# A feed-forward product of twin tiles in seven half products, with weight sums kept in DRAM

## The chip, the cores and the metric

One core of a Trainium2 chip runs the whole program; the metric is the device time of one execution in microseconds, and the median of several executions stands for a kernel. The core's engines are TensorE (matrix products into eight PSUM banks), VectorE and ScalarE (elementwise work), GpSimd (elementwise work) and SyncE, whose queue issues nearly all transfers between DRAM and SBUF. They run side by side and wait for each other by semaphores.

## The reference

Attention with a decay runs in blocks over 4 sequences of 768 tokens with 8 heads of 64; its output, 3072 tokens by 512, goes through a feed-forward part with a squared ReLU:

```python
intra = np.einsum('bhic,bhjc->bhij', qb, kb) * Dmask[None]
intra = np.einsum('bhij,bhjd->bhid', intra, vb)
inter = np.einsum('bhid,bhde->bhie', qb * lam_pow[None], kv_state)
out[:, :, sl] = intra + inter
...
h = np.maximum(x @ w_in, 0.0)
return (h * h @ w_out).astype(np.float32)
```

x is 3072 x 512, w_in 512 x 2048, w_out 2048 x 512. All inputs and the output are 32-bit floats.

## The kernel before

The tokens are cut into 24 chunks of 128. SIZES puts them into seven tiles of 3 or 4 chunks (tiles 0, 1, 3 and 5 have 3 chunks, 384 columns; tiles 2, 4 and 6 have 4, 512 columns). A tile's feed-forward part is 16 steps, one for each block f of 128 hidden features (`ffn`). Numbers are held as a rounded high part and a remainder, both in the fp32r type, so a product of two matrices is three products: high by high, high by low, low by high. A step is

- the first product (mm1, L654): the block's input weights wih and wil by the tile's halves xs, 4 groups of 128 rows times three products, 12 matmuls into one bank;
- on ScalarE the ReLU of that bank (L668) and its square, rounded, into gh (L674); on VectorE the square once more (L677) and the remainder gl (L679);
- the second product (mm2): for each chunk gh by woh (L660), gh by wol (L661), gl by woh (L663), added over the 16 steps into one bank per chunk, which stays open for the tile.

In tiles 0 and 1 ScalarE squares in place (L671) and rounds with a cast (L672), and VectorE has the one subtraction. Buffers gh and gl exist twice. When a tile ends, its banks are copied to ob rows (L697) and stored (L699).

The weights come once, 32 pieces of 512 KB (L366), are turned from 64-bit to 32-bit floats on ScalarE and VectorE (L368 to L375) and split into their two halves; they then stay in SBUF. That work goes on beside tile 0 and the beginning of tile 1. Attention for chunks 6 to 23 is done in ten *visits* (VISITS: tile, step, steps ahead), a run of some 250 small matmuls (L393) that finishes two old chunks and opens two new ones between two steps of a tile; L410 loads q, k and v of a chunk. A finished chunk's result is scaled on VectorE into xr and split into the halves xs (L500, L501).

No engine's order is left to chance: a planner (`Plan.order`) takes operations with an estimated duration, a key (a due time), their dependences and the buffers they need, and puts each engine's instructions out in the order of its own simulation; each engine runs its queue in that order.

## Time and profile before

| | us |
|---|---|
| median of 3 executions | 597.36 |
| fastest and slowest of them | 597.3, 597.68 |
| span of the profiled execution | 596.8 |
| TensorE busy in it (share) | 590.8 (99%) |
| VectorE busy | 292.0 (49%) |
| ScalarE busy | 214.1 (36%) |
| GpSimd busy | 5.4 (1%) |

The span is what one profiled execution shows from its first to its last instruction; the median is measured without the profiler and is 0.6 us longer. In the profile, L12 stands for line 12 of the kernel, PE is TensorE, PEld its weight loads, DVE VectorE, ACT ScalarE, POOL GpSimd, and SP or SPq the queue of SyncE. Matmuls are pipelined and their single durations overlap, so the length of a step is read from the starts of steps. Busy time of an engine off the chain of waits costs nothing by itself.

### The profile page before, as it was taken

What the parts mean: (1) busy time and instruction counts of PE and PEld (TensorE: products, weight loads), DVE (VectorE), ACT (ScalarE), POOL (GpSimd) and SP (SyncE); (2) the same over time, 40 slices, a digit from 0 to 9 for tenths busy, and PEclk for the clock granted to TensorE, in tenths of its full rate; (3) what the DMA queues carried; (4) which work ended last, traced back from release to release, by engine and by line L of the source; (5) the groups of instructions that cost most, each with busy time, mean ns of one, the idle gap of its engine ahead of it and who ended that gap; (6) DMA issues with size and microseconds to landing.
All of it is one profiled execution on the core that took longest, in us unless ns stands there. A gap on an engine that the chain in (4) does not pass through costs nothing.

```text
span 596.8 us, 11701 instructions
## 1 busy us (share of the span) xinstructions
PE 590.8 (99%) x5097; PEld 512.7 (86%) x5097; DVE 292.0 (49%) x551; ACT 214.1 (36%) x427; POOL 5.4 (1%) x10
## 2 busy tenths in 40 slices
PE   8999999999999999999999999999999999999997
PEld 7789898999888888889899888888889998888885
DVE  6999999954563525332624433532232524313223
ACT  5876677653342222223322222221222322222122
POOL 3000000000000000000000000000000000000000
PEclk9999999999999999999999999999999999999999
DMA  8775444505450304001403010300010000100001
GB/s 331 293 260 176 142 158 160 177 1 195 143 193 12 136 0 144 0 22 50 144 0 128 15 54 0 144 0 1 0 72 0 3 0 2 53 1 0 1 0 71
DMA packets 15171, 48.99 MB, mean 82 GB/s; under 512 B 1809, under 2 KB 1809, under 8 KB 15121
## 3 DMA queue, kind: packets, MB, share of 16 engines
q1 hardware_dynamic: 14976, 48.24, 22.7%
q8 instruction: 40, 0.66, 0.4%
q14 instruction: 11, 0.08, 0.0%
q10 hardware_dynamic: 144, 0.01, 0.0%
HBM read 41.95 MB, written 6.29 MB: 81 GB/s over the span
## 4 chain that ended last, share of the span: by engine, by line
PE 95%; DMA 4%; SPq 0%; issue 0%; DVE 0%
PE bank L654 44%; PE bank L660 15%; PE bank L661 15%; PE bank L663 15%; PE bank L393 7%; DMA ka<-ka 2%; DMA qv<-qv 2%; PE bank L637 0%; SPq L410 0%; DVE work L697 0%; SPq L366 0%
## 5 line engine op out<-in xcount | busy, mean ns | idle before, releaser
L654 PE MATMUL bank<-xs,wih 128*128 128x384 f32 (+1 forms) x888 | 193.2, 359 | 0.5 <-issue 0.5
L654 PEld LDWEIGHTS bank<-xs,wih 128*128 128x128 f32 x888 | 161.0, 188 | 19.7 <-issue 1.0
L677 DVE TENSOR_TENSOR work<-work 128x512 f32<-128x512 f32 (+1 forms) x79 | 50.4, 638 | 231.8 <-ACT gh L674 231.8
L668 ACT ACTIVATE work<-bank 128x512 f32<-128x512 f32 (+1 forms) x86 | 47.4, 551 | 285.5 <-PE bank L654 234.9
L660 PE MATMUL bank<-woh,gh 128*128 128x512 f32 x381 | 149.7, 393 | 0.0
L661 PE MATMUL bank<-wol,gh 128*128 128x512 f32 x381 | 148.6, 390 | 0.0
L654 PE MATMUL bank<-xs,wil 128*128 128x384 f32 (+1 forms) x444 | 105.2, 359 | 0.0
L663 PE MATMUL bank<-woh,gl 128*128 128x512 f32 x336 | 92.4, 390 | 0.0
L654 PEld LDWEIGHTS bank<-xs,wil 128*128 128x128 f32 x444 | 80.6, 188 | 7.5
L660 PEld LDWEIGHTS bank<-woh,gh 128*128 128x128 f32 x381 | 71.5, 188 | 14.0
L661 PEld LDWEIGHTS bank<-wol,gh 128*128 128x128 f32 x381 | 71.5, 188 | 13.2
L663 PEld LDWEIGHTS bank<-woh,gl 128*128 128x128 f32 x336 | 62.9, 188 | 13.0
L679 DVE TENSOR_TENSOR gl<-work,gh 128x512 fp32r<-128x512 f32 (+1 forms) x87 | 55.0, 632 | 17.3 <-ACT gh L672 10.4
L674 ACT ACTIVATE gh<-work 128x512 fp32r<-128x512 f32 (+1 forms) x79 | 46.6, 590 | 2.5
L393 PE MATMUL bank<-qv,ka 64*64 64x64 f32 (+2 forms) x1040 | 26.5, 225 | 0.4 <-DMA qv<-qv 0.3
L393 PEld LDWEIGHTS bank<-qv,ka 64*64 64x64 f32 (+2 forms) x1040 | 23.7, 140 | 3.0 <-DMA qv<-qv 1.1
L373 DVE SCALAR_TENSOR_TENSOR work<-work 128x512 uint32<-128x512 uint32 x30 | 20.7, 690 | 0.4
L375 DVE SCALAR_TENSOR_TENSOR work<-work 128x512 uint32<-128x512 uint32 x30 | 20.7, 690 | 0.3
L668 ACT ACTIVATE ob<-bank 128x384 f32<-128x384 f32 (+1 forms) x25 | 12.4, 496 | 22.2 <-PE bank L654 21.2
L368 ACT ACTIVATE work<-work 128x512 f32<-128x512 f32 x30 | 20.2, 674 | 0.0
L500 ACT CAST xs<-xr 128x512 fp32r<-128x512 f32 x15 | 9.3, 620 | 17.4 <-DVE xr L493 15.2
L433 DVE TENSOR_TENSOR qv<-qv,wdec 128x512 f32<-128x512 f32 (+2 forms) x20 | 11.2, 562 | 8.5 <-DMA qv<-qv 8.3
(95 smaller groups left out, 401.5 us busy)
## 6 DMA issues: line engine op xcount, KB each, us to landing
work<-w SPq DMA_DIRECT2D x32, 512.0 KB, 3.5
ka<-ka SPq DMA_DIRECT2D x24, 512.0 KB, 5.2
qv<-qv SPq DMA_DIRECT2D x20, 512.0 KB, 5.7
out<-ob SPq DMA_DIRECT2D x16, 256.0 KB, 2.3
out<-work SPq DMA_DIRECT2D x8, 256.0 KB, 2.5
work<-qv SPq DMA_DIRECT2D x4, 512.0 KB, 6.7
ob<-lamx ACTq DMA_DIRECT2D x1, 10.0 KB, 4.5
```

The source lines that it names most:

```text
L368: o = add("ACT", 0.13 + act(n), lambda cs=cs: nc.scalar.activation(at(m)[:, cs], words(1, cs).bitcast(F32), AF.Abs), [o], [st, m])
L373: o = add("DVE", tt(n), lambda cs=cs: nc.vector.scalar_tensor_tensor(out=bits(cs), in0=words(1, cs), scalar=0xC0000000, in1=bits(cs), op0= ...
L375: om.append(add("DVE", tt(n), lambda cs=cs: nc.vector.scalar_tensor_tensor(out=bits(cs), in0=words(0, cs), scalar=29, in1=bits(cs), op0=AL ...
L393: nc.tensor.matmul(*args, **kw, skip_group_check=True)
L654: nc.tensor.matmul(at(h)[:, 0:n], wt[:, cc, :], xt[:, cc, :], start=k == 0, stop=k == 3 * NCC - 1)
L660: nc.tensor.matmul(at(os_[j]), at(gh)[:, sl], woh[f], start=f == 0 and ti >= SINGLE, stop=False)
L661: nc.tensor.matmul(at(os_[j]), at(gh)[:, sl], wol[f], start=False, stop=False)
L663: nc.tensor.matmul(at(os_[j]), at(gl)[:, sl], woh[f], start=False, stop=f == NF - 1)
L668: orr = plan.op("ACT", 0.49 * to - 0.03 * (nt > 3), key, lambda: nc.scalar.activation(raw(), at(h)[:, 0:n], AF.Relu), [o1], [h, g, run])
L674: ogh = plan.op("ACT", 0.525 * to - 0.03 * (nt > 3), key, lambda: nc.scalar.activation(high(), raw(), AF.Square), [orr], [g, gh])
L677: og = plan.op("DVE", 0.07 + n / 770, key, lambda: nc.vector.tensor_tensor(out=square(), in0=raw(), in1=raw(), op=ALU.mult), [orr] + [ogh] ...
L679: ogl = plan.op("DVE", 0.07 + n / 770, key, lambda: nc.vector.tensor_tensor(out=low(), in0=square(), in1=high(), op=ALU.subtract), [og, og ...
```

## The change

SIZES keeps the first three tiles (10 chunks). The other 14 chunks become two *twins*: the first has 3 pairs of chunks (narrow, 384 columns a side), the second 4 pairs (wide, 512 columns). One twin covers two former tiles, and two feature blocks are taken together. The first product of such a pair of blocks for both sides is a 2 by 2 product: features f0 and f1, sides a and b, with the 512 rows in two halves of 256. It is done in Strassen's way (Winograd's form) with seven products of half the rows, six matmuls each (ORDER gives their sequence, `product`), and sums of their results: z11 and z12 are blocks f0 and f1 for side a, z21 and z22 for side b (`run`). ScalarE copies a result out of its bank (`copy`, after's L841), VectorE adds the next bank to it (`plus`, L844).

The sums of the inputs that a twin needs are made by VectorE when a pair of chunks is ready (`pairs`) and split like the chunks. The sums of the weights are made once, by GpSimd (`differences`): for a pair of blocks two additions of high and low part (L766, 128 x 512) and four subtractions (L775, 128 x 256), in a row, then a cast to the high part on ScalarE (L777) and the remainder on VectorE (L778). The seven moving parts per pair of blocks (three of them plain weight halves) are stored in a DRAM tensor, kept, 256 KB each (L762), and every product of both twins loads its own back into one of six buffers (`load`, L825). So 56 parts, 14.7 MB, are stored, and each is read twice.

z11 and z12 are squared at once (`whole`) and their second products follow in the next round of the same first half of the twin. z21 and z22 are squared in place and kept in SBUF (`put`); a second half of the twin casts them again (`kept_half`, L910, L911) and does their second products (L891, L892, L894), with nothing but visits between. Six visits stay in tiles 1 and 2; four lie in the twins (INSIDE). Tile 2 now squares like tiles 0 and 1 (L731, L733, L734). SBUF is laid out by hand, since the twins' buffers lie where earlier ones were (REGIONS, ERAS; `Plan.follow` adds the dependences), and gh and gl still exist twice. The work of the ten visits, the conversion of the weights and tiles 0 and 1 are otherwise left as they were.

```diff
-SIZES = [3, 3, 4, 3, 4, 3, 4]
-WIDE, NARROW = max(SIZES) * C, min(SIZES) * C
+SIZES = [3, 3, 4]
+TWINS = [3, 4]
+WIDE, NARROW = 4 * C, 3 * C
...
+VISITS = [(1, 9, 0), (1, 12, 1), (1, 14, 0), (2, 5, 0), (2, 9, 0), (2, 13, 0)]
+INSIDE = {("first", 0, 6): 6, ("second", 0, 1): 7, ("second", 0, 5): 8, ("second", 0, 9): 9}
...
+ORDER = [1, 2, 6, 5, 7, 4, 3]
+KEPT = {1: 0, 2: 1, 5: 2, 4: 3, 7: 4, 6: 5, 3: 6}
...
-        if ti < 2:
-            og = plan.op("ACT", 0.525, key, lambda: nc.scalar.activation(raw(), raw(), AF.Square), [orr], [g])
-            ogh = plan.op("ACT", 0.515, key, lambda: nc.scalar.copy(high(), raw()), [og], [g, gh])
-        else:
-            ogh = plan.op("ACT", 0.525 * to - 0.03 * (nt > 3), key, lambda: nc.scalar.activation(high(), raw(), AF.Square), [orr], [g, gh])
-            sq = Buf("xr9") if last else g
-            square = (lambda: at(sq).rearrange("p c i -> p (c i)")[:, 0:n]) if last else raw
-            og = plan.op("DVE", 0.07 + n / 770, key, lambda: nc.vector.tensor_tensor(out=square(), in0=raw(), in1=raw(), op=ALU.mult), [orr] + [ogh] * (not last), [g] + [sq] * last)
-        gsq, square = (sq, square) if ti >= 2 else (g, raw)
-        ogl = plan.op("DVE", 0.07 + n / 770, key, lambda: nc.vector.tensor_tensor(out=low(), in0=square(), in1=high(), op=ALU.subtract), [og, ogh], [gsq, gh, gl])
...
+        og = plan.op("ACT", 0.525 * to - 0.03 * (nt > 3), key, lambda: nc.scalar.activation(raw(), raw(), AF.Square), [orr], [g])
+        ogh = plan.op("ACT", 0.515 * to - 0.03 * (nt > 3), key, lambda: nc.scalar.copy(high(), raw()), [og], [g, gh])
+        ogl = plan.op("DVE", 0.07 + n / 770, key, lambda: nc.vector.tensor_tensor(out=low(), in0=raw(), in1=high(), op=ALU.subtract), [og, ogh], [g, gh, gl])
...
+    def differences(j, key):
+        f0, f1 = 2 * j, 2 * j + 1
+        raws, gate, (ws0, ws1) = [Buf("ob"), Buf("ob")], [steps[1, NF - 1][0]], (ws[f0][0], ws[f1][0])
+        flat = lambda a: a.rearrange("p c f -> p (c f)")
+        stored[j] = []
+        def store(a, c, n, get, deps, bufs, uses):
+            stored[j].append(plan.op("SP", LOAD, key, lambda: nc.sync.dma_start(out=kept[j][:, :, c:c + n].rearrange("p t c k -> p t (c k)"), in_=get().bitcast(F32)), deps, bufs, lat=2.9, uses=uses))
+        store(f0, 0, 2, lambda: wi[f0].rearrange("p t c f -> p t (c f)"), ws0[:2], [], (f"wi{f0}",))
+        store(f1, 6, 1, lambda: wi[f1].rearrange("p t c f -> p t (c f)")[:, :, 2 * P:], ws1[:2], [], (f"wi{f1}",))
+        both = [plan.op("POOL", 1.3, key, lambda r=r, f=f: nc.gpsimd.tensor_tensor(
+            out=at(r), in0=flat(wih[f]).bitcast(F32), in1=flat(wil[f]).bitcast(F32), op=ALU.add), list(w[:2]), [r], gate, uses=(f"wi{f}",))
+            for r, f, w in zip(raws, (f0, f1), (ws0, ws1))]
+        def side(r, k):
+            return at(raws[r])[:, k * 2 * P:(k + 1) * 2 * P]
+        prev = both
+        for c, (out_, a, b) in zip((2, 4, 5, 3), (((0, 0), (1, 0), (0, 0)), ((1, 0), (1, 1), (1, 0)), ((1, 1), (1, 1), (0, 0)), ((0, 1), (0, 1), (1, 1)))):
+            o = plan.op("POOL", 0.7, key, lambda out_=out_, a=a, b=b: nc.gpsimd.tensor_tensor(out=side(*out_), in0=side(*a), in1=side(*b), op=ALU.subtract), prev, raws)
+            part = Buf("part")
+            oh = plan.op("ACT", act(256), key, lambda part=part, out_=out_: nc.scalar.copy(at(part)[:, 0], side(*out_)), [o], [raws[out_[0]], part])
+            ol = plan.op("DVE", tt(256), key, lambda part=part, out_=out_: nc.vector.tensor_tensor(
+                out=at(part)[:, 1], in0=side(*out_), in1=at(part)[:, 0], op=ALU.subtract), [oh], [raws[out_[0]], part])
+            store(None, c, 1, lambda part=part: at(part), [oh, ol], [part], ())
+            prev = [o]
...
+        oa = split("a", xa_, slice(0, 4), ca.o_xr)
+        oz = split("z", xb_, hi, cb.o_xr)
+        o1 = add((xb_, hi), (xb_, lo), (xb_, hi), ALU.add, oz)
+        o3 = add((xb_, lo), (xa_, lo), (xb_, lo), ALU.subtract, o1 + ca.o_xr)
+        o2 = add((xa_, lo), (xb_, hi), (xa_, lo), ALU.subtract, o3 + oa)
+        split("t", xb_, slice(0, 4), o3 + o1)
+        o4 = add((xa_, hi), (xa_, hi), (xa_, lo), ALU.subtract, o2)
+        split("s", xa_, slice(0, 4), o4)
...
+        where = {1: "x", 2: "y", 6: "x", 5: "v", 7: "x", 4: "z", 3: "v"}
...
+        def load(i):
+            b = Buf(f"b{p}")
+            o = plan.op("SP", LOAD, key - 12 + 0.1 * ORDER.index(i), lambda: nc.sync.dma_start(out=at(b).bitcast(F32), in_=kept[j][:, :, KEPT[i]]), stored[j], [b], lat=3.2)
+            return b, o
+        def product(i, deps=()):
+            b, o = load(i)
+            k, (g, _) = where[i], moving(p, i)
+            def fn():
+                x, first = moving(p, i)[1], i in (1, 2, 5, 4)
+                for t, (u, v) in enumerate(((0, 0), (0, 1), (1, 0))):
+                    for kb in range(2):
+                        mm(psum(k), at(b)[:, u, kb * P:kb * P + P], x[:, v, kb], start=first and not t and not kb, stop=t == 2 and kb == 1)
+            return link(plan.op("PE", 6 * (n / 2400 + 0.0135), key, fn, [o] + ready2[p][g] + list(deps), [b, banks[k], x2[p]], mode="F", entries=12, uses=(f"p{p}{g}",)))
...
+        def whole(b, o):
+            get, gh, gl = lambda: at(b), Buf("gh"), Buf("gl")
+            o = squared(get, o, [b])
+            oh = plan.op("ACT", act(n) + 0.1, key, lambda: nc.scalar.activation(at(gh)[:, 0:n], get(), AF.Square), [o], [b, gh])
+            o = plan.op("DVE", 0.07 + n / 770, key, lambda: nc.vector.tensor_tensor(out=get(), in0=get(), in1=get(), op=ALU.mult), [oh], [b])
+            ol = plan.op("DVE", 0.07 + n / 770, key, lambda: nc.vector.tensor_tensor(out=at(gl)[:, 0:n], in0=get(), in1=at(gh)[:, 0:n], op=ALU.subtract), [o, oh], [b, gh, gl])
+            return gh, gl, oh, ol
+        def put(name, f, o):
+            get = lambda: later_g[p][f]
+            o = squared(get, o, [], (name,))
+            late_g[p, f] = plan.op("ACT", act(n) + 0.1, key + 1, lambda: nc.scalar.activation(get(), get(), AF.Square), [o], [], uses=(name,))
+        def run(name):
+            if name == 1:
+                st["r1"] = copy("x", r[0], product(1))
+            if name == 2:
+                st["g"] = [whole(r[0], plus("y", lambda: at(r[0]), r[0], [product(2), st["r1"]], [r[0]]))]
+            if name == 6:
+                st["r2"] = copy("x", r[1], product(6, [st["r1"]]))
+            if name == 5:
+                st["p5"] = product(5)
+            if name == 7:
+                st["r3"] = copy("x", r[2], product(7, [st["r2"]]))
+                o = st["z22"] = plus("v", lambda: later_g[p][2 * j + 1], r[2], [st["p5"], st["r3"]], [r[2]], (g1,))
+                put(g1, 2 * j + 1, o)
+            if name == 4:
+                put(g0, 2 * j, plus("z", lambda: later_g[p][2 * j], r[2], [product(4), st["r3"]], [r[2]], (g0,)))
+            if name == 3:
+                st["g"].append(whole(r[1], plus("v", lambda: at(r[1]), r[1], [product(3, [st["z22"]]), st["r2"]], [r[1]])))
...
+    def kept_half(p, f, key):
+        n, name, gh, gl = TWINS[p] * C, f"g{p}_{f}", Buf("gh"), Buf("gl")
+        oh = plan.op("ACT", act(n) + 0.1, key, lambda: nc.scalar.copy(at(gh)[:, 0:n], later_g[p][f]), [late_g[p, f]], [gh], uses=(name,))
+        ol = plan.op("DVE", 0.07 + n / 770, key, lambda: nc.vector.tensor_tensor(out=at(gl)[:, 0:n], in0=later_g[p][f], in1=at(gh)[:, 0:n], op=ALU.subtract), [oh], [gh, gl], uses=(name,))
+        return gh, gl, oh, ol
...
+    for j in range(NF // 2):
+        differences(j, begin[2] + per[2] * (2 * j + 1))
...
+            run, st = twin(p, j, key, link)
+            follow = [fn for fns in waiting for fn in fns]
+            waiting = []
+            places = {2: 2, 6: 3, 7: 4} if ("first", p, j + 1) not in INSIDE else {2: 1, 6: 2, 3: 4}
+            at_most = 0
+            for i in ORDER:
+                run(i)
+                while follow and at_most < places.get(i, 0) and len(follow):
+                    follow.pop(0)()
+                    at_most += 1
+                if i in places:
+                    at_most = places[i]
+            while follow:
+                follow.pop(0)()
+            for k, g in enumerate(st["g"]):
+                waiting.append(second_products(2 * j + k, g, os_, key, link, j + k == 0, j == NF // 2 - 1 and k == 1, nt)[:2])
...
+        for f in range(NF):
+            key = b + (c - b) * f / NF
+            v = INSIDE.get(("second", p, f))
+            if v is not None:
+                linked(visiting(v, nt == 3, key))
+            high, low, each = second_products(f, kept_half(p, f, key), os_, key, link, f == 0, f == NF - 1, nt)
+            if f < NF - 1:
+                high(), low()
```

*ScalarE in tile 2.* Before, a run of steps, two instructions each, on banks of 512 columns (work is the buffer between):

```order
L668 ACTIVATE work<-bank_66 128x512
L674 ACTIVATE gh_105<-work 128x512
L668 ACTIVATE work<-bank_63 128x512
L674 ACTIVATE gh_106<-work 128x512
L668 ACTIVATE work<-bank_67 128x512
L674 ACTIVATE gh_105<-work 128x512
L668 ACTIVATE work<-bank_61 128x512
```

The same engine after, with the casts of the weight sums (part is the buffer from which they are stored, ob the one in which GpSimd leaves them):

```order
L777 CAST part_181<-ob_102 128x256
L777 CAST part_179<-ob_103 128x256
L777 CAST part_180<-ob_103 128x256
L731 ACTIVATE work<-bank_62 128x512
L733 ACTIVATE work<-work 128x512
L777 CAST part_181<-ob_102 128x256
L734 CAST gh_99<-work 128x512
L731 ACTIVATE work<-bank_60 128x512
L733 ACTIVATE work<-work 128x512
L777 CAST part_179<-ob_103 128x256
```

The steps have three instructions in place of two, and casts of GpSimd's sums stand between them in ScalarE's queue.

*TensorE in a step of 384 columns.* Before, in tile 3, a second product (banks 67, 61 and 62 are the three chunks) and the next first product:

```order
L660 MATMUL bank_62<-woh_974,gh_106 128x512
L661 MATMUL bank_62<-wol_975,gh_106 128x512
L663 MATMUL bank_67<-woh_974,gl_108 128x512
L663 MATMUL bank_61<-woh_974,gl_108 128x512
L663 MATMUL bank_62<-woh_974,gl_108 128x512
L654 MATMUL bank_65<-xs,wih_976 128x384 x8
L654 MATMUL bank_65<-xs,wil_977 128x384 x4
```

After, a round in the narrow twin: the names b_0 to b_5 are the six buffers for the loaded parts of kept, p0t, p0z, p0s and p0a the sums of the inputs (products 5, 7, 4, 3 of one pair of blocks, then 1 and 2 of the next):

```order
L457 MATMUL bank_58<-p0t,b_0_157 128x384 x6
L457 MATMUL bank_62<-p0t,b_1_158 128x384 x6
L894 MATMUL bank_61<-wo_87,gl_100 128x512
L894 MATMUL bank_64<-wo_87,gl_100 128x512
L894 MATMUL bank_60<-wo_87,gl_100 128x512
L457 MATMUL bank_63<-p0z,b_2_159 128x384 x6
L457 MATMUL bank_58<-p0s,b_3_160 128x384 x6
L457 MATMUL bank_59<-p0a,b_4_161 128x384 x6
L457 MATMUL bank_65<-p0a,b_5_162 128x384 x6
L891 MATMUL bank_61<-wo_88,gh_98 128x512
```

The 12 matmuls on one bank gave way to products of 6 on different banks; products 5 and 3 use the same bank (here bank_58), with three low matmuls and product 4 between them and product 7 ahead of those.

*TensorE at the end of the narrow twin's first half*, after the change (wo_96 and wo_97 are blocks 14 and 15):

```order
L457 MATMUL bank_59<-p0z,b_0_157 128x384 x6
L457 MATMUL bank_58<-p0s,b_1_158 128x384 x6
L891 MATMUL bank_61<-wo_96,gh_98 128x512
L892 MATMUL bank_61<-wo_96,gh_98 128x512
L891 MATMUL bank_64<-wo_96,gh_98 128x512
L892 MATMUL bank_64<-wo_96,gh_98 128x512
L891 MATMUL bank_60<-wo_96,gh_98 128x512
L892 MATMUL bank_60<-wo_96,gh_98 128x512
L894 MATMUL bank_61<-wo_96,gl_100 128x512
L894 MATMUL bank_64<-wo_96,gl_100 128x512
L894 MATMUL bank_60<-wo_96,gl_100 128x512
L891 MATMUL bank_61<-wo_97,gh_98 128x512
```

Both blocks of the last pair use gh_98, and no product stands between them; ScalarE's queue has the cast of the first kept half into gh_99 far ahead of its use.

## Rows read from the trace of the kernel before

**Rows 1.** Page: span; TensorE and VectorE busy tenths in 40 slices of 14.9 us.

```profile
span 596.8 us, 11701 instructions
...
PE   8999999999999999999999999999999999999997
...
DVE  6999999954563525332624433532232524313223
```

**Rows 2.** Waits of TensorE: what waits, for what, total us, times, longest.

```profile
PE bank L316 <- DVE ob L300: 1.5, 1, 1.5
...
PE bank L393 <- DMA qv<-qv: 0.3, 1, 0.3
```

**Rows 3.** Chain of waits in time order: start us, us, what.

```profile
83.43 2.08 PE bank L654 x12
87.57 2.08 PE bank L654 x12
...
171.38 5.45 PE bank L654 x24
...
190.43 3.92 PE bank L393 x240
...
372.17 2.72 PE bank L654 x12
```

**Rows 4.** Windows, tile 2; columns: five engines busy (count), PEclk, DMA share, GB/s.

```profile
171.00:232.00 61.00, 61.00 (x730) 51.21 (x729) 27.45 (x51) 16.08 (x30) 0.00 (x0) 1.00 0.23 78
```

**Rows 5.** Timeline: TensorE, ScalarE, VectorE, tile 3; start us, length, what, [idle].

```profile
306.31 0.86 PE L654 MATMUL bank<-xs,wil 128*128 128x384 f32 x4
307.00 1.55 PE L654 MATMUL bank<-xs,wih 128*128 128x384 f32 x8
...
307.20 0.49 ACT L668 ACTIVATE work<-bank 128x384 f32<-128x384 f32 x1 [5.12 <-PE bank L654]
307.73 0.53 ACT L674 ACTIVATE gh<-work 128x384 fp32r<-128x384 f32 x1
...
308.29 0.56 DVE L677 TENSOR_TENSOR work<-work 128x384 f32<-128x384 f32 x1 [4.95 <-ACT gh L674]
```

**Rows 6.** ScalarE by line and shape: busy us, mean ns, idle before.

```profile
L674 ACT ACTIVATE gh<-work 128x512 fp32r<-128x512 f32 x47 | 29.8, 634 | 1.5
L668 ACT ACTIVATE work<-bank 128x512 f32<-128x512 f32 x47 | 28.2, 600 | 178.3 <-PE bank L654 146.5 <-DVE gl L679 31.8
...
L668 ACT ACTIVATE work<-bank 128x384 f32<-128x384 f32 x39 | 19.2, 493 | 107.2 <-PE bank L654 88.4 <-DVE gl L679 17.1 <-PE bank L661 1.7
L674 ACT ACTIVATE gh<-work 128x384 fp32r<-128x384 f32 x32 | 16.9, 527 | 1.0
```

**Rows 7.** VectorE by line and shape, columns as above.

```profile
L679 DVE TENSOR_TENSOR gl<-work,gh 128x512 fp32r<-128x512 f32 x48 | 33.2, 692 | 4.3
...
L679 DVE TENSOR_TENSOR gl<-work,gh 128x384 fp32r<-128x384 f32 x39 | 21.7, 558 | 13.0 <-ACT gh L672 10.4
...
L468 DVE TENSOR_TENSOR hold<-hold,lc 128x256 f32<-128x256 f32 x14 | 5.9, 420 | 0.0
```

**Rows 8.** GpSimd by line and shape, columns as above.

```profile
L306 POOL TENSOR_SCALAR_AFFINE_SELECT tri<-tri 128x128 f32<-128x128 f32 x1 | 0.3, 294 | 0.0
```

**Rows 9.** Page, part 6: DMA issues, count, KB each, us to landing.

```profile
work<-w SPq DMA_DIRECT2D x32, 512.0 KB, 3.5
...
out<-ob SPq DMA_DIRECT2D x16, 256.0 KB, 2.3
...
work<-qv SPq DMA_DIRECT2D x4, 512.0 KB, 6.7
```

**Rows 10.** Waits of the DMA queue (SP), columns as in rows 2.

```profile
SPq L366 <- DVE work L375: 81.9, 27, 6.5
```

**Rows 11.** Windows, the end and the weight loads; columns as in rows 4.

```profile
585.00:597.00 12.00, 8.11 (x36) 6.38 (x34) 2.98 (x5) 2.41 (x4) 0.00 (x0) 1.00 0.24 87
2.00:30.00 28.00, 27.64 (x353) 22.99 (x353) 22.44 (x46) 19.73 (x62) 4.68 (x4) 1.00 0.88 332
```

More of the change, by code (lines that the diff above doesn't have):

```diff
@@ L249 @@
-    make(ps, ("bank",))
-    wih, wil, woh, wol = ([None] * NF for _ in range(4))
-    def make_weights(pool, fs):
-        for f in fs:
-            for part, shape, name in ((wih, [P, NCC, P], "wih"), (wil, [P, NCC, P], "wil"), (woh, [P, DM], "woh"), (wol, [P, DM], "wol")):
-                part[f] = pool.tile(shape, F32R, name=f"{name}{f}")
-    make_weights(const, range(F_LATE))
-    make(const, [k for k in SLOTS if k not in ("bank", "x", "xb", "gl0", "run") + EARLY + WORK + AFTERWARDS])
-    work = const.tile([P, 4608], F32, name="work")
+    tiles = {}
@@ new lines @@
+    tiles["bank"] = [ps.tile([P, 512], F32, name=f"bank{i}") for i in range(SLOTS["bank"])]
+    wi = [place(f"wi{f}", REGIONS[f"wi{f}"][0], [2, NCC, P], F32R) for f in range(NF)]
+    wo = [place(f"wo{f}", 1024 * f if f < F_LATE else DYN + 21120 + 1024 * (f - F_LATE), [2, DM], F32R) for f in range(NF)]
+    wih, wil, woh, wol = [a[:, 0] for a in wi], [a[:, 1] for a in wi], [a[:, 0] for a in wo], [a[:, 1] for a in wo]
+    at_ = make("gh", 9216, [WIDE], F32R)
+    at_ = make("gl", at_, [WIDE], F32R)
@@ L690, in ffn @@
         steps[ti, f] = (o1, o2, o3)
         if f == NF - 1:
[L692 to L700 removed]
+            finish(TILES[ti], os_, [o3] * nt, ["ob9" if j == 2 else "ob" for j in range(nt)], key)
@@ new lines, in second_products, with fn, high, low @@
+    def second_products(f, g, os_, key, link, first, last, nt):
+        gh, gl, oh, ol = g
+        def fn(part, j):
+            sl = slice(j * C, (j + 1) * C)
+            if part == 0:
+                nc.tensor.matmul(at(os_[j]), at(gh)[:, sl], woh[f], start=first, stop=False)
+                nc.tensor.matmul(at(os_[j]), at(gh)[:, sl], wol[f], start=False, stop=False)
+            else:
+                nc.tensor.matmul(at(os_[j]), at(gl)[:, sl], woh[f], start=False, stop=last)
+        def high():
+            return link(plan.op("PE", 0.455 * nt, key, lambda: [fn(0, j) for j in range(nt)], [oh] + list(ws[f][1][:2]), [gh] + os_, mode="F", entries=4 * nt))
+        def low():
+            return link(plan.op("PE", 0.2275 * nt, key, lambda: [fn(1, j) for j in range(nt)], [ol], [gl, gh] + os_, mode="F", entries=2 * nt))
+        def each():
+            return [link(plan.op("PE", 0.6825, key, lambda j=j: [fn(0, j), fn(1, j)], [oh, ol], [gh, gl] + os_[j:], mode="F", entries=6)) for j in range(nt)]
+        return high, low, each
@@ L713, with place_of @@
     xs_, ready = [Buf(("x", "xb")[ti % 2]) for ti in range(len(TILES))], [[] for _ in TILES]
+    x2, ready2, stored, late_g = [Buf("xp") for _ in TWINS], [{} for _ in TWINS], {}, {}
+    def place_of(v):
+        if v < len(VISITS):
+            k, f, _ = VISITS[v]
+            return begin[k] + per[k] * f
+        which, p, n = next(k for k, i in INSIDE.items() if i == v)
+        return twice[p][0] + (twice[p][1] - twice[p][0]) * n / (NF // 2) if which == "first" else twice[p][1] + (twice[p][2] - twice[p][1]) * n / NF
     chunks = []
@@ L768 @@
         for o in done:
-            if o.late and not opened:
-                assert not early, "an earlier buffer is still in use"
-                late()
-                opened = True
+            assert not (o.late and early), "an earlier buffer is still in use"
             o.fn()
```

244 lines of the change are left out of this document (185 added, 59 removed), and 5 rows, old and new, of the table SLOTS.

## The prediction

> **What bounds the kernel now.** I read the slices of the page first: TensorE is busy in nine tenths or more of every slice but the first and the last [rows 1]. The waits say the same from the other side: TensorE waits for another engine for 1.8 us in all, and for a DMA once [rows 2]. The chain of waits is therefore a list of TensorE steps, and a step's length can be read off it: twelve matmuls of 384 columns take 2.08 us, 173 ns each, and the next such step begins 4.14 us later; twelve of 512 columns take 2.72 us, 227 ns each [rows 3]. [...] So the time is TensorE's work at a known price per matmul, and what takes matmuls away pays in full as long as nothing new makes TensorE wait.
>
> **What is removed.** For two feature blocks and a pair of tiles the first product was 4 times 12 matmuls; it becomes seven half products of 6, so 42 instead of 48. There are 8 such pairs of blocks. The twin of 3 chunks saves 48 x 173 ns = 8.3 us, the twin of 4 saves 48 x 227 ns = 10.9 us: **19.2 us** [rows 3]. The second products, the attention visits (six in tiles 1 and 2, four in the twins, ten as before) and the tail of four stores stay.
>
> **What is added on TensorE's path.** A half product shares its bank with another, so copies and sums stand between products. I take 0.20 us from the start of TensorE's next step until ScalarE starts on the finished one, 0.04 to 0.1 us between the other engines, and 0.1 us back to TensorE (the last an estimate) [rows 5]; prices of the operations are in [rows 6, 7]. Product 3 goes on in the bank of product 5 and must wait until the sum after product 7 has read that bank: 0.20 + copy 0.49 + 0.05 + sum 0.56 + 0.1 = 1.40 us after product 7. In a full round the low part of an earlier second product (0.68 us, three matmuls of 227 ns) and product 4 (6 x 173 ns = 1.04 us) lie between, 1.72 us: hidden. Where that low part has been issued earlier (the first round and the two next to the visit in the narrow twin, the first in the wide one), 0.36 us show three times; wide, 0.20 + 0.60 + 0.05 + 0.69 + 0.1 = 1.64 against 1.36, once 0.28. Sum 1.4 us.
>
> The kept halves take one of the two gh buffers during the whole first half of a twin (the order shows it), so both quarters that are used at once share the other. In a round product 6 (1.04 us) covers the squaring between the two second products: 0.20 + 0.53 + 0.1 = 0.83, hidden. At the end of the half no product is left: 0.83 us narrow, 0.20 + 0.63 + 0.1 = 0.93 wide, 1.8 us together. Tile 2 now squares in place and casts on ScalarE: 0.60 + 0.63 + 0.63 instead of 0.60 + 0.63, under a cover of 5.44 us (a second product and a first one), or 2.7 us at its last step, where casts for the twin stand in between: 0.5 us there. Beyond this I allow 1.0 us for ScalarE's 32 added casts in tile 2 that meet such a step. Sum of the added waits: 1.4 + 1.8 + 0.5 + 1.0 = **4.7 us**.
>
> **GpSimd's sums** are the unknown. Each pair of blocks wants two adds of 512 columns and four subtractions of 256, each waiting for the one before, and ScalarE's casts of them stand in the queue ahead of tile 2's activations, so a late sum stops ScalarE and then TensorE. No row shows such an operation. The nearest is GpSimd's own select, 294 ns for 128 columns with one input [rows 8], which by length gives 1.18 and 0.59, 4.7 us for six; with 0.1 to 0.15 us of hand-over each I take 5.6 us a block. Below lies VectorE's price for two inputs, 0.69 and 0.42 (the first from a 512-column row, the second from a 256-column one): 3.1 us [rows 7]. Above, twice the one-input price: 9.4 + 0.6 = 10 us. In the order, blocks 1 to 7 start with tile 2 and their last cast stands in the visit behind step 10 of tile 2. Tile 2 starts at 171.4, so that visit ends its first half at 171.4 + 21 x 2.72 + an earlier visit of 3.9 = 232.4 us [rows 3]. Between blocks 1 and 2 two rows of tile 1's result pass through the same buffer, two copies and two stores one after the other: 0.6 + 2.3 + 0.7 + 2.3 and some 2 us in queues, 8 us [rows 9]. With 5.6: 171.4 + 8 + 7 x 5.6 = 218.6, 14 us early. With the 3.2 us that a step in tile 2 can give (5.44 less 2.2), it costs nothing up to (232.4 + 3.2 - 179.4) / 7 = **8.0 us a block**; every microsecond above costs 7.
>
> [...]
>
> **Transfers.** Fourteen megabytes are stored and read back twice. Sixteen of the stores (6.3 MB) join the weight loads of the start; the order puts each behind the low part of its own block and ahead of a load that waits for a later VectorE instruction, and those loads wait for VectorE anyway, 27 times, 81.9 us in all, not for the DMA engines [rows 10]. So the stores only share the engines: 512 KB at 332 GB/s are 1.6 us [rows 11], against a load that takes 3.5 us [rows 9] and is wanted some 6 us after its issue, since two pieces of about 3 us go before it (32 pieces, in the slices with VectorE at nine tenths, up to about 120 us [rows 1, 9]): hidden, at most 1 us. A loaded half sum (256 KB) has one of six buffers: from the end of one product to the start of the sixth after it pass at least 11.4 - 2 x 1.04 - 2.04 = 7.2 us of a narrow round (42 x 173 ns + 18 x 227 ns = 11.4). A 512 KB load alone lands in 3.5 us, the last of four together in 6.7 [rows 9]. As to rate, a 2 KB packet takes 0.24 x 12 us x 16 engines / 510 = 90 ns [rows 11]; if the 1 KB packets here cost as much, seven loads are 7 x 16 x 90 ns = 10.1 us of 11.4. Hidden at both ends, 0 to 2 us.
>
> VectorE carries more in the narrow twin's second half: three visits, four sets of pair sums and sixteen low parts come to about 36 us by the prices above, of some 44 us. Tight, not over: 0 to 2 us.
>
> **Sum.** On the profiled execution [rows 1]: 596.8 - 19.2 + 4.7 = 582.3 us of span; the median of the runs lies 0.6 us above the span, so **582.9 us**. With all bounds at their good end it is 597.4 - 19.2 = 578.2. With 1 us in the start, 2 for loads and 2 on VectorE it is 588.
>
> **Rivals.** First, *GpSimd and VectorE shut each other out*. VectorE is busy for 27.5 of 61 us in 171 to 232 us [rows 4], so an operation of either often meets one of the other. If they exclude each other, a block lasts its 5.6 us plus VectorE's part in it, four splits of 0.42 and 1.5 low parts of 0.69, and as much again from the visits and the pair sums: up to 8.3 to 9 us, 2 to 7 us beyond the limit: 585 to 590. [...] GpSimd is idle in the trace from 15 us on, so no run here shows it yet. [...]
>
> Second, *each product pays for its wait*. A product begins with a wait for a DMA. If the hand-over costs 0.1 us on TensorE, 112 of them take 11 us: 594. Against it: in the trace of before the second product waits for ScalarE and the next matmul still starts on the beat [rows 3, 5].
>
> Third, on the other side, *GpSimd sets the pace of tile 2*. If the two-input price is the upper one and the exclusion comes on top, a block takes 10 + 1 to 2 us; at 11.5 the stage is 7 x 3.5 = 24 us longer and the time 607. From 10.1 us a block the gain is gone. For it: ScalarE's queue has no way round a late sum. Against it: the one-input row is half that price.
>
> Fourth, *the loads set the pace*: only if a 1 KB packet took over 100 ns, while a 4 KB one takes 0.88 x 28 us x 16 / 2270 = 174 ns [rows 11]; at 130 ns a narrow round grows to 14.6 us, 8 x 3.2 = 25 us, and the time is 608.
>
> **How the numbers follow.** Forecast (579 to 586) 0.62; exclusion 0.14; waits at products 0.08; GpSimd's pace 0.10; loads 0.02; gains eaten to within a measurement's 0.2% 0.04. The range goes from 578.2 to 592: it holds the first two and half of the third. Faster by over 0.2% 0.84, within it 0.04, slower 0.12; 0.2% is about what a measurement of this kernel can tell from no change.
>
> **What would show it.** Right: in the twins twelve matmuls keep 2.08 and 2.72 us, TensorE's waits in all are 3 to 6 us, most of them on ScalarE at the end of a half and on VectorE at product 3; GpSimd's adds take about 1.2 us and its last one ends before 225 us. Wrong: ScalarE idles for GpSimd in tile 2 and TensorE behind it (first and third rival), TensorE's waits name the loads of kept (fourth), or the first matmul of each product is late with nothing to wait for (second).

## The result: 590.8 us, less than half of the forecast gain

The changed kernel takes 590.76 us (median of 4, 589.73 to 592.99) against 597.33 us before; the ratio is 0.989, interval 0.987 to 0.992. Forecast were 582.9 us: the sign and the range held, but of 14.4 us only 6.6 came.

The page of the profiled execution: span and counts; busy tenths of TensorE, VectorE and GpSimd in 40 slices; the queue that carries instructions (packets, MB).

```profile
span 588.1 us, 12243 instructions
...
PE 574.6 (98%) x5001; PEld 495.5 (84%) x5001; DVE 341.7 (58%) x641; ACT 281.4 (48%) x569; POOL 54.2 (9%) x58
...
PE   8999999999999989999999999989999999999997
...
DVE  6899999965574596818433363876333333334222
...
POOL 3000000003045657000000000000000000000000
...
q8 instruction: 39, 0.64, 0.4%
```

Against [rows 1], 96 matmuls are gone as planned (5097 to 5001 on the two pages), but two slices of TensorE that were full are not. The waits of TensorE, as in [rows 2]:

```profile
PE bank L457 <- issue: 3.5, 2, 2.5
PE bank L457 <- DMA qv<-qv: 2.0, 3, 0.9
PE bank L457 <- ACT part L777: 1.5, 1, 1.5
...
PE bank L892 <- issue: 0.3, 1, 0.3
...
PE bank L457 <- DVE g L844: 0.2, 1, 0.2
```

The largest entry names nobody ("issue"), and its line, L457, is that of the visits' small matmuls (products share it). The waits for qv lie in the first 30 us. None names the loads of kept (L825). The chain around the longest one (start us, us, what) shows a visit of 240 matmuls, which [rows 3] has at 3.92 us, stand still for 2.55 us near its end:

```profile
387.34 3.44 PE bank L457 x220
390.77 2.55 issue
393.32 1.04 PE bank L457 x16
394.36 0.72 PE bank L891
395.08 0.43 PE bank L892
```

Behind it the matmuls take 0.43 us in place of 0.23. In the windows (columns as in [rows 4]) the granted clock there is 0.53, against 1.00 ahead of it; TensorE had done nothing for 2.3 us:

```profile
391.00:393.30 2.30, 0.00 (x0) 0.00 (x0) 1.38 (x3) 1.00 (x2) 0.00 (x0) 1.00 0.01 3
393.30:396.00 2.70, 2.68 (x22) 2.27 (x22) 1.60 (x4) 0.00 (x0) 0.00 (x0) 0.53 0.03 6
```

By the starts of the steps, three visits took 5.63, 5.74 and 7.02 us (at 207, 235 and 387 us) where the others of 240 to 256 matmuls took 3.89 to 4.02. The 1.5 us that the waits put down to ScalarE's cast (L777) are the gap in the first of these three. All visits from 137 us on took 42.6 us, before 36.0.

### The profile page after: what moved, and what is told of

The parts are those of the page before. It is cut to its first block, busy times and chain, and to the rows that moved or that the text cites. A ratio compares the mean times of both kernels' runs of the same rounds, so it can differ in the third digit from the quotient of the medians.

```text
span 588.1 us, 12243 instructions
## 1 busy us (share of the span) xinstructions
PE 574.6 (98%) x5001; PEld 495.5 (84%) x5001; DVE 341.7 (58%) x641; ACT 281.4 (48%) x569; POOL 54.2 (9%) x58
## 4 chain that ended last, share of the span: by engine, by line
PE 87%; DMA 5%; DVE 4%; issue 2%; ACT 1%; POOL 0%; SPq 0%; ACTq 0%
PE bank L457 28%; PE bank L717 16%; PE bank L891 9%; PE bank L892 9%; PE bank L894 9%; PE bank L723 5%; PE bank L724 5%; PE bank L726 5%; DMA ka<-ka 2%; DMA qv<-qv 2%; DVE part L778 0%; DMA kept<-part 0%; DVE xa L565 0%; DVE g L844 0%; ACT r L841 0%
## 5 line engine op out<-in xcount | busy, mean ns | idle before, releaser
L891 PE MATMUL bank<-wo,gh 128*128 128x512 f32 x224 | 88.7, 396 | 0.0
L892 PE MATMUL bank<-wo,gh 128*128 128x512 f32 x224 | 87.9, 393 | 0.3 <-issue 0.3
L717 PE MATMUL bank<-xa,wi 128*128 128x512 f32 (+1 forms) x372 | 79.5, 365 | 0.2 <-DVE xa L565 0.2
L717 PEld LDWEIGHTS bank<-xa,wi 128*128 128x128 f32 x372 | 67.6, 188 | 9.5 <-DVE xa L565 0.6
L723 PE MATMUL bank<-wo,gh 128*128 128x512 f32 x157 | 61.9, 395 | 0.0
L894 PE MATMUL bank<-wo,gl 128*128 128x512 f32 x224 | 61.8, 390 | 0.0
L724 PE MATMUL bank<-wo,gh 128*128 128x512 f32 x157 | 61.3, 390 | 0.0
L841 ACT COPY r<-bank 128x384 f32<-128x384 f32 (+1 forms) x48 | 25.5, 532 | 68.3 <-PE bank L457 68.3
L844 DVE TENSOR_TENSOR g<-bank,r 128x384 f32<-128x384 f32 (+1 forms) x32 | 19.9, 625 | 61.2 <-ACT r L841 57.8
L891 PEld LDWEIGHTS bank<-wo,gh 128*128 128x128 f32 x224 | 42.4, 189 | 9.7 <-ACT gh L853 0.7
L892 PEld LDWEIGHTS bank<-wo,gh 128*128 128x128 f32 x224 | 42.5, 190 | 8.2
L894 PEld LDWEIGHTS bank<-wo,gl 128*128 128x128 f32 x224 | 42.0, 188 | 8.5 <-DVE gl L855 0.2
L911 DVE TENSOR_TENSOR gl<-g,gh 128x384 fp32r<-128x384 f32 (+1 forms) x32 | 19.9, 623 | 34.0 <-PE bank L894 32.0
L766 POOL TENSOR_TENSOR ob<-wi 128x512 f32<-128x512 f32 x16 | 22.1, 1385 | 175.1 <-ACT work L731 127.2
L910 ACT CAST gh<-g 128x384 fp32r<-128x384 f32 (+1 forms) x32 | 18.2, 568 | 41.6 <-PE bank L892 41.5
L735 DVE TENSOR_TENSOR gl<-work,gh 128x512 fp32r<-128x512 f32 (+1 forms) x23 | 20.4, 889 | 28.9 <-ACT gh L734 26.7
L844 DVE TENSOR_TENSOR r<-bank,r 128x384 f32<-128x384 f32 (+1 forms) x32 | 20.0, 624 | 28.5 <-PE bank L457 27.9
L717 PE MATMUL bank<-xb,wi 128*128 128x384 f32 x192 | 35.2, 336 | 0.0
L717 PEld LDWEIGHTS bank<-xb,wi 128*128 128x128 f32 x192 | 33.6, 188 | 0.9
L723 PEld LDWEIGHTS bank<-wo,gh 128*128 128x128 f32 x157 | 29.5, 188 | 5.7
L724 PEld LDWEIGHTS bank<-wo,gh 128*128 128x128 f32 x157 | 29.5, 188 | 5.2
```

The lines of the kernel that those rows point to most:

```text
L717: nc.tensor.matmul(at(h)[:, 0:n], wt[:, cc, :], xt[:, cc, :], start=k == 0, stop=k == 3 * NCC - 1)
L723: nc.tensor.matmul(at(os_[j]), at(gh)[:, sl], woh[f], start=f == 0 and ti >= SINGLE, stop=False)
L724: nc.tensor.matmul(at(os_[j]), at(gh)[:, sl], wol[f], start=False, stop=False)
L735: ogl = plan.op("DVE", 0.07 + n / 770, key, lambda: nc.vector.tensor_tensor(out=low(), in0=raw(), in1=high(), op=ALU.subtract), [og, ogh], ...
L766: both = [plan.op("POOL", 1.3, key, lambda r=r, f=f: nc.gpsimd.tensor_tensor(out=at(r), in0=flat(wih[f]).bitcast(F32), in1=flat(wil[f]).bi ...
L841: return plan.op("ACT", act(n) + 0.09, key - 6, lambda: nc.scalar.copy(at(dst), psum(k)), [o], [banks[k], dst])
```

## The experiments

Two theories stood at first. **F**: TensorE's instructions themselves come over the DMA engines (the 39 packets on the page above), and the new transfers delay them. **G**: the visits wait for ScalarE, VectorE or a bank, because sums and casts fill the queues. After the first four runs came **A**, alignment. The kernel before ran again beside each group: 597.9, 598.1 and 597.8 us.

**e1_loads_once** uses each of the six buffers again instead of loading anew:

```diff
+            k = (p, ORDER.index(i) % 6)
+            if k in loaded_once:
+                return loaded_once[k]
```

> Each of the six buffers for parts of kept is loaded once per twin (12 loads in place of 112) and used again by the later products, so their values are not the reference's; every engine but the DMA queue keeps its order. Theory F (program reading): TensorE's instructions come from DRAM in blocks of 256, a visit uses up two blocks in 4 us, and when the loads fill the DMA engines the next block is late; then TensorE stands still for something that the profile cannot name. It expects the visit that takes 7.0 us at 387 us to take 4.0 to 4.3 us, the granted clock behind it to stay at 1.00, and the span to fall from 588.1 by 3.5 to 4.5 us, to about 584; the two visits of tile 2 (5.6 and 5.7 us) stay. Theory G (VectorE, ScalarE or a bank comes late in the visit) expects 7.0 us again and a span of 588.

Measured 586.38 us, ratio 0.980 (0.978 to 0.982). The visit took 5.41 us, not 4.0 to 4.3; its gap was 1.28 us, and the matmuls behind it ran at their usual price. The six first loads still lay beside the visit, which the expectation overlooked, so this run decides less than it was meant to. Five of them were issued within about 1 us of their places beside the visit in the changed kernel, so with the same loads the gap can be half as long. It shows that the other hundred loads cost no beat: the products' waits are the same.

**e2_no_sums** stores plain weights in place of the sums:

```diff
-            o = plan.op("POOL", 0.7, key, lambda out_=out_, a=a, b=b: nc.gpsimd.tensor_tensor(out=side(*out_), in0=side(*a), in1=side(*b), op=ALU.subtract), prev, raws)
...
+            store(f, c, 1, lambda f=f: wi[f].rearrange("p t c f -> p t (c f)")[:, :, 2 * P:], [steps[1, NF - 1][0]], [], (f"wi{f}",))
```

> GpSimd's sums, their casts on ScalarE and their remainders on VectorE are left out; the 32 stores stay and copy plain weights into kept, so the values are not the reference's. Theory F: the two visits of tile 2 still lose time as long as stores and loads run beside them, over 4.5 us each. Theory G: both take 4.0 us, the span falls by 3.3 us to about 585. Both expect the start of tile 2 to lose its 0.5 us and ScalarE to wait for GpSimd no more (13.1 us before).

Measured 586.98 us, ratio 0.982 (0.979 to 0.985); the visits took 5.20, 5.07 and 6.06 us. Its waits:

```profile
PE bank L457 <- issue: 4.0, 4, 1.9
```

With no sum and no cast of one left in tile 2, gaps of 1.02 and 0.82 us stayed there, both under "issue", the first at the same matmul as the wait for L777 in the changed kernel to within one. G falls as the main cause. The span, 585.2 us, is about what G named, but only 1.1 us of the 2.9 came from the two visits; the visit at 387 us was 1.0 us shorter, though nothing beside it had been left out, and the clock stayed at 1.00 behind it.

**e3_no_part_stores** makes the sums but doesn't store them:

```diff
-            store(None, c, 1, lambda part=part: at(part), [oh, ol], [part], ())
```

> The sums are made, cast and split as in the changed kernel, but the 32 stores of them (256 KB each) are left out; all loads read the three stored weight parts of their pair of blocks, so the values are not the reference's. Theory F: the two visits of tile 2 take 4.0 to 4.4 us in place of 5.6 and 5.7, the span falls by 2.5 to 3.3 us, to about 585. Theory G: they stay at 5.6 and 5.7, the span at 588. The visit at 387 us stays at about 7 us in both.

Measured 590.24 us, ratio 0.988 (0.984 to 0.991): the visits of tile 2 took 7.08 and 5.16 us, 12.2 us together against 11.4 in the changed kernel, where F had expected 8.0 to 8.8. F in its first form, transfers alone, falls too. (In the first of the two, 2.25 us of the wait are put down to ScalarE's copy L517 and 0.5 to VectorE.) The visit at 387 us, which both theories expected at about 7 us, took 5.14, with a gap of 1.02 us and the loads beside it.

**e4_loads_behind_visit** lets the wide twin's loads wait for the first matmul behind the visit:

```diff
+        if p:
+            tc.add_manual_dep(d.ins, mark[-1], mybir.DependencyInfo(mybir.DependencyClass.Sync, mybir.DependencyReason.DATA), reason="visit")
```

> Nothing is left out. The loads for the wide twin wait until the last but one visit (387 us) has gone by; before, five of them were issued between 380 and 388.5 us. Theory F: that visit takes 4.0 to 4.3 us in place of 7.0, the clock behind it stays at 1.00, and the span falls by 3.5 to 4.5 us to about 584, with a spread between runs as small as before the change (0.6 us). Theory G: the visit stays at 7 us. If the loads then come too late for the wide twin, its first products start late by up to 3 us and the gain is gone.

Measured 586.46 us (585.73 to 587.18), ratio 0.981 (0.978 to 0.983). The time came out about as F said (the span by 2.6 us shorter, 3.5 to 4.5 were expected), the visit didn't: it took 5.29 us, with a gap of 1.17 us and no transfer beside it but these. Windows (columns as in [rows 4], the last two are the DMA engines' share and GB/s):

```profile
387.50:389.50 2.00, 2.00 (x133) 1.94 (x136) 0.97 (x2) 0.28 (x3) 0.00 (x0) 1.00 0.00 0
...
389.75:390.00 0.25, 0.25 (x32) 0.25 (x24) 0.25 (x1) 0.25 (x1) 0.00 (x0) 1.00 0.29 66
390.00:391.00 1.00, 1.00 (x71) 0.92 (x63) 1.00 (x4) 0.34 (x1) 0.00 (x0) 1.00 0.00 0
391.00:392.25 1.25, 0.08 (x7) 0.01 (x3) 1.25 (x4) 0.15 (x1) 0.00 (x0) 1.00 0.00 0
...
393.25:393.50 0.25, 0.25 (x3) 0.20 (x2) 0.25 (x2) 0.00 (x0) 0.00 (x0) 1.00 0.31 66
```

66 GB/s for 0.25 us are 16.5 KB, and so is 0.64 MB over 39 packets on the page: 5001 matmuls and 5001 weight loads are 256 instructions for each packet. By this count the traffic is TensorE's program. The trace then says where a block ends, by counting matmuls: the gaps at 212.1 and 240.5 us in the changed kernel lie 383 matmuls apart, those at 379.7 and 393.3 lie 255 apart, one less than three and two times 128. (TensorE's stream has 88 semaphore instructions too. In e1 it has 38, and there the gap at 387 us came 11 matmuls later, as if they took places in the blocks.) That is theory A: ordinary steps use up a block in 27 to 29 us (the packets of the kernel before lie at 527, 554 and 583 us), a visit in 2.0 us.

In the kernel before, the same packets beside the visit at 227 us:

```profile
225.50:225.75 0.25, 0.25 (x3) 0.21 (x2) 0.00 (x0) 0.25 (x1) 0.00 (x0) 1.00 0.25 66
...
229.75:230.00 0.25, 0.25 (x32) 0.25 (x22) 0.25 (x2) 0.18 (x1) 0.00 (x0) 1.00 0.27 66
```

Here the first block end lies about 10 matmuls into the visit, yet its packet starts at 225.7 us, 1.4 us ahead of the visit, so TensorE's queue seems to be read some way ahead of what is executed, and 4.1 us lie between the two packets. By the count it was so in most visits of the kernel before; in the changed one the first block end lies about 65, 111 and 95 matmuls into the three long visits and 13, 7 and 3 into three that cost nothing. Three things to try follow: shift the blocks, move the visits, part a visit.

**e5_before_shifted**, the kernel before with 64 more instruction pairs where TensorE idles anyway (35 small matmuls for three fillers; the trace shows each of these as two):

```diff
+        if 2 <= count[0] < 5:
+            for k in range(35 * (count[0] == 2)):
+                h = half(k % 2)
+                nc.tensor.matmul(tiles["bank"][i][h, 0:HC], zero[h, 0:HC], zero[h, 0:HC], start=True, stop=True)
+            return
```

> The kernel before the change, where three filler matmuls in the idle first microseconds are replaced by 35 small ones that take about as long: 64 more instructions pairs on TensorE, nothing else; every other instruction keeps its place. Theory A (alignment): TensorE's program is read in blocks of 256 instructions, the block after next is asked for when one is entered, and takes some 3.5 us until it can be used. A visit uses 256 instructions in 2 us, so it stalls where two block ends lie inside it and not where the first falls into the first 17 matmuls or so. In the kernel before, the block ends lie 12 to 17 matmuls into five of the visits and so cost nothing; shifted by 64 they lie at 76 and 204. A expects seven visits (at 150, 190, 227, 285, 319, 377 and 464 us) to take 1.0 to 1.8 us longer each, and the time to grow by 8 to 12 us, to about 607. Theory F as first put (only transfers delay a block) and theory G (queues) expect no change: 597.

Measured 608.94 us, ratio 1.018 (1.016 to 1.019): 10.8 us slower with all other instructions in place. Its waits, and the chain through the visit that [rows 3] shows at 190.43 us:

```profile
PE bank L401 <- issue: 8.1, 8, 1.4
```

```profile
193.18 3.21 PE bank L401 x201
196.39 1.37 issue
197.76 1.02 PE bank L401 x38
```

The seven named visits took 0.8 to 1.7 us longer, and an eighth, at 165 us, has a gap too; in the one shown the gap comes after 201 matmuls, 204 were expected.

**e6_after_shifted**, the changed kernel shifted by 52 in the same way (28 small matmuls for two fillers).

> The changed kernel with 52 more instruction pairs on TensorE at the start, in place of two fillers. Theory A: the block ends move 52 matmuls forward in every visit: at 207 us from 65 to 13 (5.6 us becomes 4.0 to 4.2), at 235 from 111 to 59 (stays over 5), at 387 from 95 to 43 (stays over 5), and the visits that were at 13, 7 and 3 (263, 340 and 374 us) get two block ends inside and take 1.0 to 1.8 us longer each; so does the one at 150. In sum 2 to 4 us slower: 592 to 595. Theories F and G expect all visits as in the changed kernel and 590 to 591.

Measured 594.35 us, ratio 0.993 (0.991 to 0.995). The visit at 207 us took 4.14 us; those that had cost nothing took 5.07, 5.23 and 5.34 us (263, 340 and 374 us), the one at 150 us 4.72, and those at 235 and 387 us stayed long, 5.86 and 5.49. The named visits went as A said, but for the one at 150 us, which grew by 0.7 us and not by 1.0 to 1.8; one at 165 us (5.13 us) hadn't been named.

```profile
267.37 3.44 PE bank L465 x218
270.81 0.82 issue
271.63 0.81 PE bank L465 x35
```

**e7_visits_at_2_8** moves two visits of tile 2 by a few steps of 24 matmuls:

```diff
-VISITS = [(1, 9, 0), (1, 12, 1), (1, 14, 0), (2, 5, 0), (2, 9, 0), (2, 13, 0)]
+VISITS = [(1, 9, 0), (1, 12, 1), (1, 14, 0), (2, 2, 0), (2, 8, 0), (2, 13, 0)]
```

> Two visits of tile 2 go back to the steps that they had before the change, from steps 5 and 9 to 2 and 8; a step has 24 matmuls, so the block ends move from 65 and 111 matmuls into the visit to 9 and 7. Theory A: both take 4.0 to 4.2 us in place of 5.6 and 5.7, the time falls by 3 us to about 587.5; the visit at 387 us stays at 6 to 7 us. Theory G (GpSimd's sums and the casts in ScalarE's queue make them late): they stay as long, or get longer, since more of the sums lie beside and behind them.

Measured 586.31 us, ratio 0.980 (0.978 to 0.983); the visits took 3.92 and 4.04 us. The visit at 387 us, which A expected at 6 to 7 us, took 5.43 with the loads beside it; its gap is the second line. A new wait came, the first line:

```profile
PE bank L723 <- ACT gh L734: 2.1, 1, 2.1
...
PE bank L457 <- issue: 1.3, 1, 1.3
```

At 205 us ScalarE stood 2.5 us before a cast, whose buffer was still being stored, with tile 2's own cast (L734) behind it. That is the place which the third rival named, but a store that hadn't landed held it, not a sum.

**e8_visit_split** parts the visit at 387 us around a second product:

```diff
+                if v == 8:
+                    linked(chain[2:])
```

> In the narrow twin's second half the visit at 387 us is parted in the middle: the second product that stood behind it (9 matmuls, 2.04 us) now stands between its first two pieces and its last two. The block ends stay at 95 and 223 matmuls into the visit, but 2 us more lie between them. Theory A: the two pieces take 4.0 to 4.3 us together, nothing of the 2.55 us gap is left, the clock behind it stays at 1.00, the time falls by 3.5 to 4.3 us to about 586.8. Theory F (transfers alone): the loads are still there and at least half of the gap stays, or moves to the next block end.

Measured 585.75 us, ratio 0.979 (0.978 to 0.981), with the loads still beside it:

```profile
387.04 2.02 PE bank L457 x128
...
391.33 1.44 PE bank L457 x85
392.77 0.29 issue
393.06 0.81 PE bank L457 x27
```

2.04 us more between two block ends leave 0.29 us of 2.55, where A had expected nothing to be left.

**e9_aligned** puts e4, e7 and e8 together.

> The changes of e4_loads_behind_visit, e7_visits_at_2_8 and e8_visit_split together; nothing is left out. Theory A: no visit loses more than 0.4 us to a block end; against e7 (586.3) the visit at 387 us loses 1.5 us less, so 584.5 to 585.0; the 2.1 us that tile 2 waits at 205 us for ScalarE's cast, which stands behind a store, stay. If the forecast's terms were otherwise right, 597.4 - 19.2 + 2.0 (product 3) + 0.5 (gh) + 0.5 (start of tile 2) + 2.1 = 583.3.

Measured 583.86 us, ratio 0.977 (0.976 to 0.979): somewhat better than expected, since the wait at 203 us shrank to 0.7 us by itself:

```profile
PE bank L723 <- ACT gh L734: 0.7, 1, 0.7
```

**e10_aligned_replanned** also tells the planner what GpSimd and the stores really take:

```diff
-plan.op("POOL", 1.3, key
+plan.op("POOL", 1.6, key
...
-in_=get().bitcast(F32)), deps, bufs, lat=2.9, uses=uses))
+in_=get().bitcast(F32)), deps, bufs, lat=4.5, uses=uses))
```

> e9_aligned, with longer durations for GpSimd's sums (1.6 and 1.0 us in place of 1.3 and 0.7) and for the landing of their stores (4.5 us in place of 2.9) in the planner, so that it puts the casts later in ScalarE's queue. Expected: the 2.1 us wait at 205 us goes or shrinks to under 0.5, and the time falls by 1.5 to 2.1 us against e9_aligned, to 582 to 583. Theory G, by which the sums pace tile 2 wherever the casts stand, expects the wait at another step and the time of e9_aligned.

Measured 582.88 us (582.69 to 583.14), ratio 0.975 (0.974 to 0.977), the best of all, 1.0 us below e9 where 1.5 to 2.1 were expected: the wait that it was to remove was only 0.7 us in e9. Its span and waits:

```profile
span 581.1 us, 12245 instructions
```

```profile
PE bank L457 <- DMA qv<-qv: 1.6, 3, 0.7
PE bank L378 <- DVE ob L362: 1.5, 1, 1.5
PE bank L901 <- issue: 0.2, 1, 0.2
PE bank L457 <- DVE g L851: 0.2, 1, 0.2
```

The waits for qv and ob lie in the first 30 us. Tile 2 waits for nobody now, so G's form of the third rival falls: the casts' place in the queue was what mattered.

## Why the prediction was wrong, by its own steps

**What is removed**: right. In the changed kernel's chain twelve matmuls still take 2.08 and 2.72 us, and 96 are gone: 19.2 us.

**"The attention visits ... stay"**: this is the step that failed. Their matmuls stayed and were costed at nothing; that the program comes in packets, and where the block ends fall, was not looked at, though the page of before has the queue of instructions on it (40 packets, 0.66 MB), and its waits have one such gap, at 292.95 us, which [rows 2] leave out:

```profile
PE bank L654 <- issue: 0.5, 1, 0.5
```

Every edit ahead of a visit (96 matmuls fewer, visits at other steps) moves those ends. It cost 6.6 us in the visits. The clock behind the longest gap took 1.3 us more (six matmuls at 0.43 in place of 0.23 us). e5 and e6 show the cause by itself, in both kernels; e7 and e8 take it away in two independent ways. The packets say the same: the twelve traces have 42 gaps at block ends, and in 39 of them TensorE went on 2.2 to 2.8 us after the start of the packet before (3.1 to 3.4 in the other three), the one at 212.1 us, which the profile gives to ScalarE, 2.4 us after it. In e5 the packet started 0.4 to 0.9 us behind the first of the two block ends, by the count of matmuls. Transfers made it worse at one place: ahead of the 2.55 us gap the packet started 2.3 us behind the first block end, without the loads (e4) 0.8 us, and 1.17 us of the gap stay. They need not: with the same loads beside this visit the gap was 1.02 to 1.94 us in e1, e2, e3 and e7, where the packet started 0.8 to 1.1 us behind the block end; what decides this isn't shown. With these gaps, up to 1.94 us, the clock stayed at 1.00.

**Product 3**: nearly right, too low. The timeline (start us, us, what) has in the first narrow round

```profile
280.44 1.21 PE L457 MATMUL bank<-p0z,b 128*128 128x384 f32 x6
281.76 1.31 PE L457 MATMUL bank<-p0s,b 128*128 128x384 f32 x6
```

1.32 us from start to start where six matmuls take 1.04: 0.28 us late, and product 3 itself another 0.11 late at its end. This happens four times narrow, not three, and once wide: 1.95 us against 1.4. The fourth is the last round, where the three low matmuls lie in between and don't suffice.

**The shared gh**: too dear. Between the two second products at the end of a half stand three low matmuls, which the order in the section on the change shows and the sum left out: 0.83 less 0.68 is 0.15; the trace has about 0.25 us narrow and 0.1 wide, not 1.8.

**Casts in tile 2** (1.5 us): 0.5 us, at the start of the tile, where VectorE's split of xa (L565) comes late behind remainders; no later step waits.

**GpSimd's sums**: the price of an operation was near, that of a block was not (GpSimd by line and shape; VectorE in 171 to 240 us, first with the sums, then without them in e2):

```profile
L766 POOL TENSOR_TENSOR ob<-wi 128x512 f32<-128x512 f32 x16 | 22.1, 1385 | 175.1 <-ACT work L731 127.2 <-DVE part L778 45.5 <-DMA out<-ob 2.4
L775 POOL TENSOR_TENSOR ob<-ob,ob 128x256 f32<-128x256 f32 x24 | 20.5, 853 | 1.9
```

```profile
L735 DVE TENSOR_TENSOR gl<-work,gh 128x512 fp32r<-128x512 f32 x11 | 12.7, 1159 | 5.0 <-ACT gh L734 4.7
...
L524 DVE TENSOR_TENSOR work<-bank,hold 128x256 f32<-128x256 f32 x4 | 1.7, 416 | 0.4 <-PE bank L457 0.4
```

```profile
L735 DVE TENSOR_TENSOR gl<-work,gh 128x512 fp32r<-128x512 f32 x11 | 7.6, 692 | 35.8 <-ACT gh L734 35.8
...
L524 DVE TENSOR_TENSOR work<-bank,hold 128x256 f32<-128x256 f32 x4 | 1.7, 424 | 4.4 <-PE bank L457 4.4
```

1.39 and 0.85 us against 1.18 and 0.59. What was left out is that GpSimd waits for VectorE's remainder (L778): its two ob buffers come free only behind the casts and remainders. Of the 45.5 us, 26.6 lie ahead of 170.6 us and 18.9 inside the stretch of blocks 1 to 7, which lasts from 170.6 to 235.9 us, 9.3 us a block. The prediction set 8 us of such a stretch aside for the rows between blocks 1 and 2; counted so, a block took 8.2 us, just above the 8.0 that were to be free. Yet the last one ended within 0.3 us of the limit that was worked out (235.6), and no step waited; ScalarE waited 13.1 us for GpSimd where it had room.

**First rival**: its mechanism is there, and a block takes nearly the 8.3 to 9 us that it named (8.2 by that count), but TensorE pays nothing for it. VectorE's operation on two SBUF inputs takes 1159 ns in the stretch with GpSimd's sums and 692 without them (at 193.43 us, begun 0.02 us behind a sum of 1.29 us, it took 1.82), while one that reads a bank takes 416 and 424. No wait of TensorE in the changed kernel could be put down to it.

**Second and fourth rival**: neither. Products start on the beat, and no wait names the loads of kept.

The sum again, for the profiled executions: 596.8 - 19.2 + 6.6 (visits) + 1.3 (clock) + 1.95 (product 3) + 0.35 (gh) + 0.5 (start of tile 2) + 0.45 (a block end three matmuls behind the visit at 374 us) = 588.75, less 0.8 for the one block end that cost the kernel before something (at 292.95 us): 588.0, measured 588.1. The other 0.9 us of the median are runs whose mean clock was lower, 0.994 and 0.991 against 0.997, with spans of 589.9 and 591.3: the time also scatters more, 3.3 us from lowest to highest (4.0 in e3), against 0.45 us in e10; that the gaps do this isn't shown. What lies around the span was 1.7 us in each of the changed kernel's executions and some 2 us in those of before that were listed later with their spans (595.2 to 597.7 us); the 0.6 us of the prediction came of a profiled execution that, by these spans, was about 1 us longer than the median one.

That e10 comes to the predicted 582.9 us is partly luck: of its waits product 3 is dearer than forecast, gh and the casts cheaper. But it shows that the terms about the change were right within 2 us, and the missing one was in a part of the program whose instructions the change left as they were.

Left open: what makes TensorE ask for the next block was inferred from where the packets lie, not measured by itself (A's rule for it, its 3.5 us and F's word that the blocks come from DRAM are the author's theories), and so the place from which a block end begins to cost (between 15 and 43 matmuls into a visit, by the visits of these runs) is only bounded.

## What to carry to other kernels

Where a stretch of small matmuls uses instructions much faster than the rest, count them: in these kernels a visit used 256 in 2.0 us, and where two block ends lay well inside it TensorE stood still for 0.5 to 2.55 us. An edit far ahead of the stretch can shift the block ends into it: 64 instruction pairs in the first microseconds did so for eight visits (e5). Before a change is judged by its time, shift its instructions by half a block (64 pairs) at a place where the engine idles; if the time moves by more than the change, as in e5 by 10.8 us, alignment is being measured. A wait that the profile puts down to "issue" inside such a stretch, at distances of whole blocks (383 and 255 matmuls here), was the sign (the profile gave one to an engine, that at 212 us). More time between the two block ends took it away: other work in the middle left 0.29 us of 2.55 (e8), and with the first block end at the start of the stretch two visits took 3.92 and 4.04 us in place of 5.63 and 5.74 (e7).
